# The gate of a two-expert adapter mixture: from a copied tile on two engines to VectorE reading PSUM

## Chip, cores and metric

The kernel runs on one core of a Trainium2 chip. A time is the device time of the whole program in microseconds (us); the kernel before takes 125.9 us, the median of three runs (125.78, 125.90, 126.79). Profiles are of single executions on the chip; the one of the kernel before has a span of 124.6 us from its first to its last instruction.

## The reference

Two parts follow each other. The first is a gated linear recurrence over 768 steps for 4 batches and 8 heads with 48 columns each; its output, with the heads laid side by side, is x with 3072 rows of 384. The second is a mixture of low-rank adapters: each row picks 2 of 8 experts.

```python
for t in range(S):
    state = alpha[:, :, t, :, None] * state + np.einsum('bhd,bhe->bhde', k[:, :, t], v[:, :, t])
    y[:, :, t] = np.einsum('bhd,bhde->bhe', q[:, :, t], state)
...
logits = x @ w_gate                                   # [3072, 8]
topk = np.argpartition(-logits, K, axis=1)[:, :K]     # K = 2
sel = np.take_along_axis(logits, topk, axis=1)
sel = sel - sel.max(-1, keepdims=True)
w = np.exp(sel)
w /= w.sum(-1, keepdims=True) + 1e-09
...                                                   # for each expert e of a row's two
z = x[mask] @ A[e]                                    # rank 16
delta[mask] += w[mask, k, None] * (z @ B[e])
...
return x + delta
```

## The kernel before

The sequence is cut into 24 chunks of 128 steps (6 for each batch); every stage below is a function of the chunk u. A planner inside the kernel gives each stage an engine and orders all stages of all chunks, so that chunks overlap; the weights in its table LEAD steer the order, and each engine then works its instructions off in that order. The stages outside the change, in a few words:

- `ln` (ScalarE): logarithm of alpha, two chunks at a time; `cum` (TensorE): its running sums; `eup`, `edn`, `edec` (ScalarE): their exponentials
- `kgm`, `qgm`, `vbc` (GpSimd): k and q scaled by these, v cast to bf16: 128x384 for each chunk, written as `kg`, `qg`, `vb`
- `tr` (TensorE) transposes `kg` and `qg` into PSUM, `kq` (VectorE) copies them out
- `at` (TensorE): scores within the chunk; `msk` (VectorE) multiplies them by the causal mask, `at_sb`, 128x1024
- `kv` (TensorE): the state; `sdm` (VectorE) decays it into `sdec`
- `yt` (TensorE): the chunk's output transposed, `xs` (ScalarE) copies it out
- `qs`, `av` (TensorE): the output once more, not transposed, added up in the bank `y`; `delta` adds the adapters' part there, `fin` (ScalarE) copies it out as `o`, and a DMA stores it.

The gate lies between `xs` and `zt`. One product with the weights of all experts beside the gate's gives 8 x 16 adapter columns and 8 logits in one PSUM tile; the rows below follow in this order.

```python
E = 8; R = 16; P = 128; NW = E * R + E
moep = ctx.enter_context(tc.tile_pool(name="moep", bufs=3))
# PSUM: one pool whose six banks (tag "m") are handed out in turn
# to cum, tr, kv, yt, z and y/zt of all chunks
...
def z(u):
    s["z"] = ps_s.tile([P, NW], F4, name="z", tag="m", bufs=6)
    for p in range(NP):
        nc.tensor.matmul(
            s["z"], s["xs"][:, p, :], W[:, p, :], start=(p == 0), stop=(p == NP - 1))

def zc(u):                                    # L565: all of z out to SBUF
    s["zc"] = moep.tile([P, NW], F4, name="zc")
    nc.scalar.copy(s["zc"], s["z"])

def gmx(u):                                   # L570: the eight logits in descending order
    s["mx"] = moep.tile([P, 8], F4, name="mx")
    nc.vector.max(s["mx"], s["zc"][:, E * R:NW])

def gdf(u):                                   # L575: less the largest
    s["df"] = moep.tile([P, E], F4, name="df")
    nc.vector.tensor_scalar(s["df"], s["zc"][:, E * R:NW], s["mx"][:, 0:1], None, ALU.subtract)

def gex(u):                                   # L580
    s["ex"] = moep.tile([P, E], F4, name="ex")
    nc.scalar.activation(s["ex"], s["df"], AF.Exp)

def gwu(u):                                   # L586: zero below the second largest; the sum to den
    s["wu"] = moep.tile([P, E], F4, name="wu")
    s["den"] = moep.tile([P, 1], F4, name="den")
    nc.vector.scalar_tensor_tensor(
        out=s["wu"], in0=s["zc"][:, E * R:NW], scalar=s["mx"][:, 1:2], in1=s["ex"],
        op0=ALU.is_ge, op1=ALU.mult, accum_out=s["den"])

def grd(u):                                   # L593
    s["rd"] = moep.tile([P, 1], F4, name="rd")
    nc.vector.reciprocal(out=s["rd"], in_=s["den"])

def gw(u):                                    # L598: the weights
    s["w"] = moep.tile([P, E], F4, name="w")
    nc.vector.tensor_scalar(s["w"], s["wu"], s["rd"][:, 0:1], None, ALU.mult)

def gzw(u):                                   # L603: each expert's 16 columns by its weight
    s["zw"] = moep.tile([P, E, R], F2, name="zw")
    nc.gpsimd.tensor_tensor(
        out=s["zw"], in0=s["zc"][:, 0:E * R].rearrange("p (e r) -> p e r", e=E),
        in1=_bc(s["w"][:, :], R), op=ALU.mult)

def zt(u):                                    # L611: transpose into the bank of y
    bank = ps_s.tile([P, 512], F4, name="y", tag="m", bufs=6)
    s["y"], s["zt"] = bank[:, 0:DM], bank[:, DM:512]
    nc.tensor.matmul(
        s["zt"], s["zw"].rearrange("p e r -> p (e r)"), ident[:, :],
        start=True, stop=False, skip_group_check=True)

def zs(u):                                    # L618
    nc.scalar.copy(s["zs"], s["zt"])
...
```

Of the kernel before, what the change touches and what calls it, by code (L numbers as in the profile page):

```python
# [9 lines left out]
ALU = mybir.AluOpType  # L10
# [3 lines left out]
F4 = mybir.dt.float32  # L14
# [5 lines left out]
E = 8  # L20
R = 16
P = 128
NP = H // 2
HP = 64
NW = E * R + E
# [8 lines left out]
def _bc(src: bass.AP, rep: int) -> bass.AP:  # L34
    aps = [list(x) for x in src.ap]
    return bass.AP(tensor=src.tensor, offset=src.offset, ap=aps + [[0, rep]])


def _bc_mid(src: bass.AP, reps) -> bass.AP:
# [14 lines left out]
    "gdf": ("DVE", 76, 160), "gex": ("ACT", 107, 232), "gwu": ("DVE", 268, 352),  # L54
    "grd": ("DVE", 71, 155), "gw": ("DVE", 76, 160), "gzw": ("POOL", 380, 430), "zt": ("PE", 57, 220),
    "zs": ("ACT", 147, 272), "delta": ("PE", 163, 330), "fin": ("ACT", 385, 485),
    "st": ("DMA", 655, 2455),
}
LEAD = {
    "vbc": -12.82, "ln": -79.7, "cum": -86.5, "edn": -48.18, "eup": 69.81, "edec": -28.78,  # L60
    "kgm": 82.51, "qgm": -38.95, "tr": -24.18, "kq": -54.99, "sdm": -7.62, "kv": 81.99,
    "at": -3.06, "msk": 19.28, "qs": 45.2, "av": -5.12, "xb": 0.5, "xt": 0.4, "xs": 19.13,
    "z": 54.23, "zc": -33.57, "gmx": -113.64, "gdf": -52.42, "gex": 27.38, "gwu": 83.15,
    "grd": -60.48, "gw": -7.12, "gzw": 60.4, "yt": 4.05, "zt": 33.97, "zs": 72.62,
    "delta": -14.68, "fin": -30.62, "st": 100,
}
CHAINS = (
    "ln cum eup kgm tr kq at msk yt xs z zc gmx gdf gex gwu grd gw gzw zt zs delta fin st",
    "cum edn qgm tr", "cum edec sdm kv", "kgm kv", "vbc kv", "sdm yt", "kq yt",
    "vbc yt", "zt qs av delta", "zt av",  # L70
)
# [2 lines left out]
    ("tr", "qgm", QRING), ("kv", "vbc", VRING), ("av", "vbc", VRING), ("at", "kq", 5), ("av", "kq", 5),  # L74
    ("msk", "at", 1), ("av", "msk", 4), ("z", "xs", 3), ("delta", "zs", 3), ("st", "fin", 5),
    ("qs", "sdm", SRING), ("kv", "sdm", 1), ("kgm", "cum", 3), ("qgm", "cum", 3), ("at", "tr", 5),
    ("av", "tr", 5), ("z", "yt", 3), ("gzw", "z", 3), ("delta", "zt", 3), ("st", "zt", 5),
    ("edec", "kv", -1), ("qs", "kv", SRING - 1), ("delta", "gzw", 3),
)
HOLDS = {  # L80
    "cum": (("eup", 0), ("edn", 0), ("edec", 0)), "tr": (("kq", 0),), "kv": (("sdm", 1),),
    "yt": (("xs", 0),), "z": (("zc", 0),), "zt": (("fin", 0),),
}
SLOTS = 6
READER = ("ln", "kgm", "qgm", "vbc")
# [174 lines left out]
def kernel(  # L260
# [11 lines left out]
    nc = tc.nc  # L272
# [8 lines left out]
    moep = ctx.enter_context(tc.tile_pool(name="moep", bufs=3))  # L281
# [64 lines left out]
    for n in early:  # L346
# [6 lines left out]
        out=suf, in_=suf, compare_op=ALU.is_gt, fill=0.0, base=0,  # L353
# [23 lines left out]
    for i in range(SRING):  # L377
# [8 lines left out]
        out=mask, in_=mask, compare_op=ALU.is_ge, fill=0.0, base=0,  # L386
# [4 lines left out]
    st = [dict() for _ in range(NU)]  # L391
# [167 lines left out]
            nc.tensor.matmul(  # L559
                s["z"], s["xs"][:, p, :], W[:, p, :], start=(p == 0), stop=(p == NP - 1))  # L560

    def zc(u):
        s = st[u]
        s["zc"] = moep.tile([P, NW], F4, name="zc")
        nc.scalar.copy(s["zc"], s["z"])  # L565

    def gmx(u):
        s = st[u]
        s["mx"] = moep.tile([P, 8], F4, name="mx")
        nc.vector.max(s["mx"], s["zc"][:, E * R:NW])  # L570

    def gdf(u):
        s = st[u]
        s["df"] = moep.tile([P, E], F4, name="df")
        nc.vector.tensor_scalar(s["df"], s["zc"][:, E * R:NW], s["mx"][:, 0:1], None, ALU.subtract)  # L575

    def gex(u):
        s = st[u]
# [3 lines left out]
    def gwu(u):  # L582
        s = st[u]
        s["wu"] = moep.tile([P, E], F4, name="wu")
        s["den"] = moep.tile([P, 1], F4, name="den")
        nc.vector.scalar_tensor_tensor(  # L586
            out=s["wu"], in0=s["zc"][:, E * R:NW], scalar=s["mx"][:, 1:2], in1=s["ex"],
            op0=ALU.is_ge, op1=ALU.mult, accum_out=s["den"])

    def grd(u):  # L590
# [1 line left out]
        s["rd"] = moep.tile([P, 1], F4, name="rd")  # L592
        nc.vector.reciprocal(out=s["rd"], in_=s["den"])  # L593

    def gw(u):
        s = st[u]
        s["w"] = moep.tile([P, E], F4, name="w")
        nc.vector.tensor_scalar(s["w"], s["wu"], s["rd"][:, 0:1], None, ALU.mult)  # L598

    def gzw(u):  # L600
        s = st[u]
        s["zw"] = moep.tile([P, E, R], F2, name="zw")
        nc.gpsimd.tensor_tensor(  # L603
            out=s["zw"], in0=s["zc"][:, 0:E * R].rearrange("p (e r) -> p e r", e=E),
            in1=_bc(s["w"][:, :], R), op=ALU.mult)

    def zt(u):
        s = st[u]
# [22 lines left out]
    def store(u):  # L631
# [3 lines left out]

    emit = dict(
        ld=ld, wcast=wcast, ln=ln, cum=cum, eup=eup, edn=edn, edec=edec, kgm=kgm, qgm=qgm, vbc=vbc,
        tr=tr, kq=kq, sdm=sdm, kv=kv, at=at, msk=msk, qs=qs, av=av, yt=yt, xs=xs, z=z, zc=zc,
        gmx=gmx, gdf=gdf, gex=gex, gwu=gwu, grd=grd, gw=gw, gzw=gzw, zt=zt, zs=zs, delta=delta, fin=fin,
        st=store)  # L640
    for n in order:
        if n not in early:
# [31 lines left out]
```

## Time and profile before

| engine | busy us | share of the span | instructions |
|---|---|---|---|
| TensorE, matmuls | 83.1 | 67% | 1312 |
| VectorE | 84.2 | 68% | 227 |
| GpSimd | 71.5 | 57% | 121 |
| ScalarE | 69.2 | 55% | 201 |

The table gives averages over the whole span. The first products run only when the first inputs have landed, so the shares of the stretch in which all engines work are higher than these; the prediction reads them stretch by stretch. In a row of the profile's groups, a name such as `df<-zc,mx` is an output and its inputs, the numbers behind the bar are the busy time of all instances in us and the mean of one in ns, and behind the second bar stands how long the engine was idle before them, with what ended most of that time. PE is TensorE, PEld its weight loads, DVE VectorE, ACT ScalarE, POOL GpSimd, SP the engine that issues most DMAs.

### The profile page before, as it was taken

The page shows a single profiled execution, that of the slowest core. Times are in us where ns is not written, and L with a number is a line of the kernel's source. Part 1 is how long each engine was busy: PE and PEld are TensorE (multiplying, and loading weights), DVE is VectorE, ACT ScalarE, POOL GpSimd, SP SyncE. Part 2 cuts the span into 40 slices and gives each one's busy share as a digit, 9 for nine tenths or more (in the row PEclk, how much of TensorE's full clock was granted, in tenths as well). Part 3 has the DMA queues.
Part 4 walks back from the last instruction along what each step waited for, and adds up shares of the span by engine and source line. Part 5 has one row for each costly group of instructions (what it writes and reads, how often), then busy time and mean ns, then how long its engine had stood idle before and what let it go on. Part 6 is the DMA issues. An engine that isn't in the chain of part 4 may idle for free.

```text
span 124.6 us, 3448 instructions
## 1 busy us (share of the span) xinstructions
PE 83.1 (67%) x1312; PEld 64.0 (51%) x1312; DVE 84.2 (68%) x227; ACT 69.2 (55%) x201; POOL 71.5 (57%) x121
## 2 busy tenths in 40 slices
PE   0000310994798689669896899689829997797750
PEld 0000210783566478447774676468618885575520
DVE  3000000589998877985898899999984599999520
ACT  0007910363279955614888767477694684455650
POOL 7400065979609479477447789772657597740310
PEclk9999999999999968976999999999985599999997
DMA  2976988998898949498969497977895510003051
GB/s 46 282 108 157 293 250 250 272 275 214 258 248 254 264 138 295 148 253 269 266 163 302 145 254 200 296 263 216 239 303 202 186 72 0 5 0 108 24 192 63
DMA packets 32064, 24.21 MB, mean 194 GB/s; under 512 B 4272, under 2 KB 32048, under 8 KB 32048
## 3 DMA queue, kind: packets, MB, share of 16 engines
q1 hardware_dynamic: 28288, 23.60, 63.9%
q10 hardware_dynamic: 3760, 0.41, 2.4%
q8 instruction: 10, 0.16, 0.6%
q14 instruction: 6, 0.05, 0.1%
HBM read 19.28 MB, written 4.72 MB: 193 GB/s over the span
## 4 chain that ended last, share of the span: by engine, by line
DVE 34%; PE 25%; DMA 12%; ACT 10%; SPq 9%; issue 4%; ACTq 1%; POOL 1%; POOLq 0%; DVEq 0%
DVE at_sb L512 13%; SPq L305 9%; DMA a_t<-in_alpha_dram 7%; DVE df L575 5%; DMA W_st<-in_moe_A_dram 5%; PE tr L474 4%; DVE sdec L461 4%; DVE kq L480 3%; DVE wu L586 3%; ACT xs L536 2%; PE yt L528 2%; PE z L559 2%; PE y L551 2%; PE y L622 2%; PE y L542 2%
## 5 line engine op out<-in xcount | busy, mean ns | idle before, releaser
L442 POOL TENSOR_TENSOR kg<-k_t,up 128x384 bf16<-128x384 f32 x24 | 23.9, 1003 | 22.9 <-DMA k_t<-in_k_dram 11.8
L480 DVE COPY kq<-tr 128x1024 bf16<-128x1024 bf16 x24 | 16.5, 686 | 23.6 <-PE tr L474 23.3
L512 DVE TENSOR_TENSOR at_sb<-at,mask 128x1024 bf16<-128x1024 f32 x24 | 29.3, 1219 | 1.6 <-PE y L551 0.7
L449 POOL TENSOR_TENSOR qg<-q_t,dn 128x384 bf16<-128x384 f32 x24 | 24.0, 1014 | 3.5 <-ACT dn L428 2.0
L603 POOL TENSOR_TENSOR zw<-zc,w 128x128 bf16<-128x128 f32 x24 | 9.5, 403 | 19.4 <-DVE w L598 8.7
L536 ACT CAST xs<-yt 128x512 bf16<-128x512 f32 x24 | 14.0, 582 | 7.5 <-PE yt L528 7.4
L408 PE MATMUL cum<-lg,suf 128*128 128x384 bf16 x24 | 9.0, 385 | 12.4 <-ACT lg L399 12.4
L423 ACT ACTIVATE up<-cum 128x384 f32<-128x384 f32 x24 | 11.1, 495 | 10.4 <-PE cum L414 10.4
L474 PE MATMUL tr<-ident,kg 128*128 128x128 bf16 x96 | 11.1, 249 | 3.9 <-POOL kg L442 3.9
L474 PE MATMUL tr<-ident,qg 128*128 128x128 bf16 x96 | 10.8, 244 | 3.7 <-POOL qg L449 3.7
L456 POOL CAST vb<-v_t 128x384 bf16<-128x384 f32 x24 | 12.0, 519 | 1.8 <-PE y L551 1.8
L559 PE MATMUL z<-W,xs 128*128 128x136 bf16 x96 | 10.5, 236 | 3.6 <-DVE W L333 1.8
L504 PE MATMUL at<-kq 48*128 48x128 bf16 x192 | 10.2, 229 | 3.2 <-DVE at_sb L512 2.7
L629 ACT COPY o<-y 128x384 f32<-128x384 f32 x24 | 10.9, 486 | 2.4 <-PE y L622 2.3
L528 PE MATMUL yt<-at_sb,vb 128*64 128x128 bf16 x192 | 10.4, 232 | 2.3 <-DVE at_sb L512 2.1
L575 DVE TENSOR_SCALAR df<-zc,mx 128x8 f32<-128x8 f32 x24 | 11.5, 485 | 0.4
L565 ACT COPY zc<-z 128x136 f32<-128x136 f32 x24 | 6.7, 281 | 8.8 <-PE z L559 8.5
L461 DVE TENSOR_TENSOR sdec<-kv,dec 128x384 bf16<-128x384 f32 x20 | 11.0, 548 | 1.0 <-PE kv L494 1.0
L428 ACT ACTIVATE dn<-cum 128x384 f32<-128x384 f32 x24 | 11.4, 518 | 0.0
L474 PEld LDWEIGHTS <-kg 128*128 128x128 bf16 x96 | 7.4, 110 | 5.9 <-POOL kg L442 4.0
L399 ACT ACTIVATE lg<-a_t 128x768 bf16<-128x768 f32 x12 | 10.2, 858 | 0.0
L580 ACT ACTIVATE ex<-df 128x8 f32<-128x8 f32 x24 | 4.9, 212 | 8.8 <-DVE df L575 8.7
(55 smaller groups left out, 168.5 us busy)
## 6 DMA issues: line engine op xcount, KB each, us to landing
out_dram<-o SPq DMA_DIRECT2D x24, 192.0 KB, 2.5
W_st<-in_moe_A_dram ACTq DMA_DIRECT2D x8, 24.0 KB, 4.9
B_st<-in_moe_B_dram ACTq DMA_DIRECT2D x1, 192.0 KB, 4.2
a_t<-in_alpha_dram SPq DMA_DIRECT2D x4, 0.2 KB, 7.9
k_t<-in_k_dram SPq DMA_DIRECT2D x4, 0.2 KB, 9.0
q_t<-in_q_dram SPq DMA_DIRECT2D x4, 0.2 KB, 8.9
v_t<-in_v_dram SPq DMA_DIRECT2D x4, 0.2 KB, 10.7
W_st<-in_moe_w_gate_dram ACTq DMA_DIRECT2D x2, 6.0 KB, 4.1
```

The source lines that it names most:

```text
L428: nc.scalar.activation(s["dn"].rearrange("p h d -> p (h d)"), s["cum"][:, 0:DM], AF.Exp, scale=-1.0)
L442: nc.gpsimd.tensor_tensor(out=s["kg"][:, :, 0:D], in0=batches[b][1][:, c], in1=s["up"], op=ALU.mult)
L449: nc.gpsimd.tensor_tensor(out=s["qg"][:, :, 0:D], in0=batches[b][2][:, c], in1=s["dn"], op=ALU.mult)
L456: nc.gpsimd.tensor_copy(out=s["vb"][:, :, 0:D], in_=batches[b][3][:, c])
L461: nc.vector.tensor_tensor(out=sdec[u % SRING].rearrange("p a b d -> p (a b) d")[:, :, 0:D], in0=st[u - 1].pop("kv").rearrange("p a b d -> ...
L474: nc.tensor.transpose(t[:, w, p, :], pair(src, p), ident[:, :])
L480: nc.vector.tensor_copy(out=s["kq"], in_=s["tr"])
L512: nc.vector.tensor_tensor(out=s["at_sb"].rearrange("p a b t -> p (a b) t"), in0=s["at"].rearrange("p a b t -> p (a b) t"), in1=_bc_mid(mas ...
L528: nc.tensor.matmul(s["yt"][HP * hh:HP * hh + HP, p, :], s["vb"][:, 2 * p + hh, :], s["at_sb"][:, hh, p, :], start=(c == 0 and p == 0), sto ...
L536: nc.scalar.copy(s["xs"], s["yt"])
L559: nc.tensor.matmul(s["z"], s["xs"][:, p, :], W[:, p, :], start=(p == 0), stop=(p == NP - 1))
L575: nc.vector.tensor_scalar(s["df"], s["zc"][:, E * R:NW], s["mx"][:, 0:1], None, ALU.subtract)
```

## The change

VectorE reads the logits, and then the adapter columns, straight from the PSUM tile `z`. The copy `zc` on ScalarE goes. The normalised weights `w` are no longer written: the product takes the unnormalised weights `wu` and the reciprocal `rd` in one instruction, and this instruction moves from GpSimd to VectorE[...]. It is meant to shorten the gate's chain by two links and to take work from ScalarE and GpSimd. The planner holds z's bank until `gzw` instead of until `zc`, and its weights LEAD are new for nearly all stages, so the order of emission differs throughout the kernel.

```diff
-    "z": ("PE", 240, 410), "zc": ("ACT", 153, 278), "gmx": ("DVE", 91, 175),
+    "z": ("PE", 240, 410), "gmx": ("DVE", 91, 175),
...
-    "grd": ("DVE", 71, 155), "gw": ("DVE", 76, 160), "gzw": ("POOL", 380, 430), "zt": ("PE", 57, 220),
+    "grd": ("DVE", 71, 155), "gzw": ("DVE", 258, 342), "zt": ("PE", 57, 220),
...
 LEAD = {
-    "vbc": -12.82, "ln": -79.7, "cum": -86.5, ...
+    "vbc": -52.68, "ln": -26.63, "cum": 56.89, ...
...
-    "ln cum eup kgm tr kq at msk yt xs z zc gmx gdf gex gwu grd gw gzw zt zs delta fin st",
+    "ln cum eup kgm tr kq at msk yt xs z gmx gdf gex gwu grd gzw zt zs delta fin st",
...
-    "yt": (("xs", 0),), "z": (("zc", 0),), "zt": (("fin", 0),),
+    "yt": (("xs", 0),), "z": (("gzw", 0),), "zt": (("fin", 0),),
...
-    def zc(u):
-        s = st[u]
-        s["zc"] = moep.tile([P, NW], F4, name="zc")
-        nc.scalar.copy(s["zc"], s["z"])
-
...
-        nc.vector.max(s["mx"], s["zc"][:, E * R:NW])
+        nc.vector.max(s["mx"], s["z"][:, E * R:NW])
...
-        nc.vector.tensor_scalar(s["df"], s["zc"][:, E * R:NW], s["mx"][:, 0:1], None, ALU.subtract)
+        nc.vector.tensor_scalar(s["df"], s["z"][:, E * R:NW], s["mx"][:, 0:1], None, ALU.subtract)
...
-            out=s["wu"], in0=s["zc"][:, E * R:NW], scalar=s["mx"][:, 1:2], in1=s["ex"],
+            out=s["wu"], in0=s["z"][:, E * R:NW], scalar=s["mx"][:, 1:2], in1=s["ex"],
...
-    def gw(u):
-        s = st[u]
-        s["w"] = moep.tile([P, E], F4, name="w")
-        nc.vector.tensor_scalar(s["w"], s["wu"], s["rd"][:, 0:1], None, ALU.mult)
-
     def gzw(u):
         s = st[u]
         s["zw"] = moep.tile([P, E, R], F2, name="zw")
-        nc.gpsimd.tensor_tensor(
-            out=s["zw"], in0=s["zc"][:, 0:E * R].rearrange("p (e r) -> p e r", e=E),
-            in1=_bc(s["w"][:, :], R), op=ALU.mult)
+        nc.vector.scalar_tensor_tensor(
+            out=s["zw"], in0=s["z"][:, 0:E * R].rearrange("p (e r) -> p e r", e=E),
+            scalar=s["rd"][:, 0:1], in1=_bc(s["wu"][:, :], R), op0=ALU.mult, op1=ALU.mult)
```

More of the change, by code (lines that the diff above doesn't have):

```diff
@@ L59 @@
 LEAD = {
[L60 to L65, printed above, removed]
+    "vbc": -52.68, "ln": -26.63, "cum": 56.89, "edn": 39.81, "eup": 21.91, "edec": -22.93,
+    "kgm": 25.06, "qgm": -48.73, "tr": 56.8, "kq": -24.41, "sdm": -13.3, "kv": -5.97,
+    "at": 120.74, "msk": -46.64, "qs": -121.83, "av": 19.7, "xb": 0.5, "xt": 0.4, "xs": -1.32,
+    "z": -75.7, "zc": -33.57, "gmx": 36.34, "gdf": -3.62, "gex": 91.18, "gwu": -50.53,
+    "grd": 20.25, "gw": -7.12, "gzw": -11.18, "yt": -15.31, "zt": 15.28, "zs": -110.93,
+    "delta": -25.33, "fin": -73.68, "st": 100,
 }
 CHAINS = (
-    "ln cum eup kgm tr kq at msk yt xs z zc gmx gdf gex gwu grd gw gzw zt zs delta fin st",
+    "ln cum eup kgm tr kq at msk yt xs z gmx gdf gex gwu grd gzw zt zs delta fin st",
     "cum edn qgm tr", "cum edec sdm kv", "kgm kv", "vbc kv", "sdm yt", "kq yt",
@@ L76 @@
     ("qs", "sdm", SRING), ("kv", "sdm", 1), ("kgm", "cum", 3), ("qgm", "cum", 3), ("at", "tr", 5),
-    ("av", "tr", 5), ("z", "yt", 3), ("gzw", "z", 3), ("delta", "zt", 3), ("st", "zt", 5),
+    ("av", "tr", 5), ("z", "yt", 3), ("delta", "zt", 3), ("st", "zt", 5),
     ("edec", "kv", -1), ("qs", "kv", SRING - 1), ("delta", "gzw", 3),
@@ L637 @@
         ld=ld, wcast=wcast, ln=ln, cum=cum, eup=eup, edn=edn, edec=edec, kgm=kgm, qgm=qgm, vbc=vbc,
-        tr=tr, kq=kq, sdm=sdm, kv=kv, at=at, msk=msk, qs=qs, av=av, yt=yt, xs=xs, z=z, zc=zc,
-        gmx=gmx, gdf=gdf, gex=gex, gwu=gwu, grd=grd, gw=gw, gzw=gzw, zt=zt, zs=zs, delta=delta, fin=fin,
+        tr=tr, kq=kq, sdm=sdm, kv=kv, at=at, msk=msk, qs=qs, av=av, yt=yt, xs=xs, z=z,
+        gmx=gmx, gdf=gdf, gex=gex, gwu=gwu, grd=grd, gzw=gzw, zt=zt, zs=zs, delta=delta, fin=fin,
         st=store)
```

## The prediction

> **What bounds the kernel now.** I read the page's first part (busy time by engine) for the balance, then busy time by stretch for where each engine is full, then the groups for the lines the change touches, and last the timeline around their longest instances.
>
> Busy time by stretch: stretch, length, then busy us of each engine, the granted TensorE clock, the DMA share and GB/s.
>
> ```profile
> 29.00:45.00 16.00, 11.59 (x202) 8.69 (x201) 14.49 (x40) 10.46 (x32) 10.22 (x16) 0.99 0.84 238
> 45.00:60.00 15.00, 12.55 (x184) 10.09 (x183) 11.15 (x27) 7.89 (x24) 10.67 (x16) 0.79 0.75 222
> 60.00:75.00 15.00, 12.43 (x226) 9.83 (x224) 13.35 (x35) 11.84 (x37) 9.84 (x14) 1.00 0.80 233
> 75.00:90.00 15.00, 13.26 (x227) 10.06 (x225) 14.81 (x39) 10.28 (x30) 10.10 (x16) 1.00 0.82 242
> 90.00:105.00 15.00, 11.35 (x167) 9.38 (x166) 11.32 (x26) 9.79 (x30) 10.48 (x17) 0.77 0.49 164
> 105.00:119.00 14.00, 11.70 (x201) 8.50 (x198) 12.22 (x45) 7.83 (x26) 5.74 (x10) 1.00 0.11 38
> ```
>
> The engines stand in the order TensorE, its weight loads, VectorE, ScalarE, GpSimd. The first 29 us are loading and start-up, which the change does not touch. Of the 90 us that follow, 60 (29 to 45, 60 to 90, 105 to 119) have VectorE busy 14.49 + 13.35 + 14.81 + 12.22 = 54.9 us, 91%; from 75 to 90 it is full. In the other 30 us (45 to 60, 90 to 105) TensorE's clock is 0.79 and 0.77, VectorE has a quarter of its time free, and the faster thing to have would be TensorE. So VectorE sets the pace in two thirds of the steady part. The DMA queues are busy but no engine waits for a load after start-up (the list of waits has DMA only under the first loads).
>
> The groups concerned (line, engine, operation, shapes, count | busy us, mean ns | idle before, releaser):
>
> ```profile
> L575 DVE TENSOR_SCALAR df<-zc,mx 128x8 f32<-128x8 f32 x24 | 11.5, 485 | 0.4
> L603 POOL TENSOR_TENSOR zw<-zc,w 128x128 bf16<-128x128 f32 x24 | 9.5, 403 | 19.4 <-DVE w L598 8.7 <-DVE df L575 5.0 <-ACT o L629 2.0
> L586 DVE SCALAR_TENSOR_TENSOR wu<-zc,mx,ex 128x8 f32<-128x8 f32 x24 | 7.6, 326 | 3.1 <-ACT ex L580 2.9
> L565 ACT COPY zc<-z 128x136 f32<-128x136 f32 x24 | 6.7, 281 | 8.8 <-PE z L559 8.5
> L598 DVE TENSOR_SCALAR w<-wu,rd 128x8 f32<-128x8 f32 x24 | 6.2, 268 | 1.6 <-POOL zw L603 0.5
> ```
>
> The surprise is df: eight elements per partition cost 485 ns on average, though the tile's own view gives 221 as its shortest and 300 as its median. The timeline says what the long ones sit beside:
>
> ```profile
> 69.02 1.97 POOL L449 TENSOR_TENSOR qg<-q_t,dn 128x384 bf16<-128x384 f32 x2
> ...
> 70.09 0.93 DVE L575 TENSOR_SCALAR df<-zc,mx 128x8 f32<-128x8 f32 x1
> ...
> 81.30 1.04 DVE L586 SCALAR_TENSOR_TENSOR wu<-zc,mx,ex 128x8 f32<-128x8 f32 x1
> 81.31 1.00 POOL L449 TENSOR_TENSOR qg<-q_t,dn 128x384 bf16<-128x384 f32 x1
> ```
>
> Start plus duration: df ends at 71.02 and GpSimd's pair at 70.99; wu ends at 82.34 and qg at 82.31. A tiny VectorE instruction lasts until GpSimd's 1.0 us product is through. Meanwhile at_sb, kq and sdec, which read PSUM, hold to their means (1219, 686, 548 ns) at all times.
>
> [...] So df with its tensor in PSUM, and wu with one input in PSUM, should leave the lock; kq's steady 686 ns fits.
>
> [...] From at_sb (1024 elements, 1219 ns) and sdec (384, 548): (1219 − 548)/640 = 1.048 ns an element and a fixed 548 − 402 = 146 ns, from PSUM. mx at its shortest, 144 ns for 8 elements from SBUF, leaves 144 − 8 = 136. I take the 10 ns[...].
>
> [...]
>
> **The change part by part.**
>
> Removed from VectorE:
> - w, 24 times: the next instruction starts 0.14 us after w (71.90 to 72.04), 24 × 0.14 = 3.4 us, and its lock share (268 − 231 median) × 24 = 0.9 us.
> - the lock in df: (485 − 225, the unlocked length) × 24 = 6.2 us.
> - the lock in wu: (326 − 227 median) × 24 = 2.4 us.
>
> Added to VectorE: gzw, 128 elements from PSUM with a per-partition scalar. 128 × 1.048 + 146 = 280 ns; the scalar costs what df's shortest has over mx's, 221 − 144 = 77; together about 357 ns. at_sb's 1219 ns leave 1.13 us from start to start (48.97 to 50.10), 0.09 overlapped, so gzw occupies 0.27 us, × 24 = 6.5 us. PSUM surcharge: 10 ns × 72 = 0.7 us.
>
> VectorE in sum: 12.9 − 7.2 = 5.7 us less, 84.2 to about 78.5.
>
> GpSimd loses 9.5 us of work, and its in-order queue loses the 19.4 us in which zw stood at its head while the kg and qg products behind it stood too. ScalarE loses 6.7 us of zc and the 8.8 us it was idle before it. TensorE's work is unchanged. The gate's chain loses the zc link and one hand-over; z's PSUM bank, given back by zc until now, is held until gzw. The emission order is also planned afresh (other LEAD weights), which I can't price.
>
> What of it lies on the path: the four full stretches hold 20 of the 24 df, with 2.19 + 2.16 + 2.40 + 1.70 = 8.45 us, of which 8.45 − 20 × 0.225 = 3.95 is lock. With 20/24 of the rest: 3.95 + 2.0 + 3.6 − 6.0 = 3.55 us less VectorE there. TensorE has 49.0 us of those 60, so it becomes the next limit; I let three quarters through: 2.7 us. In the two slow-clock stretches VectorE isn't the bound, but the chain that ended last passes through df there in pieces of 0.65, 0.97 and 0.68 us; I give 0.4 us. In the tail, the last chunk's max starts 0.30 us earlier without zc (117.21 to 117.51), and gzw can start where w started (119.09) and end at 119.45, where zw ended at 119.87: 0.7 us together. For the longer hold of the bank I take off 0.6 us. 2.7 + 0.4 + 0.7 − 0.6 = 3.2 us: 125.9 − 3.2 = 122.7 us.
>
> **Rivals.**
>
> 1. VectorE gets fuller. Counted without locks the change adds work: 0.27 − 0.14 = +0.13 us a chunk, + 0.7 us: 3.8 us in all. If most long df and wu are waits for something else than GpSimd, or the locks fall on times when nothing hangs on VectorE, the time goes to 127 to 129. For it: VectorE is the bound. Against: the matched ends, and that the long df lie in the full stretches too.
>
> 2. The PSUM bank takes the place of the lock. Six banks are handed out in turn to cum, tr, kv, yt, z and zt; 5 × 24 + 20 = 140 tiles in 90 us, one per 0.64 us, so a bank comes round after about 3.9 us. z is held under 1 us now (71.85 to the end of its copy, 72.62). From mx to the end of w the timeline of VectorE shows 1.6 to 5.6 us, mostly near 2.4, with five chunks over 4 us. If gates stay that long, TensorE's next tile waits for gzw: several waits of 1 to 2 us, and 125 to 128. For it: in-order queues on both sides. Against: those five long gates are ones where other VectorE work was placed inside the gate, and the order is planned anew with z held until gzw.
>
> 3. TensorE, or its clock, holds the pace. It has 72.9 us of the 90 and no less work. Then the faster VectorE only makes it wait: 124.5 to 125.5. For it: the two stretches near 0.78. Against: the full clock in the other 60 us.
>
> 4. All 5.7 us and the freed GpSimd come through, with kg and qg running ahead into the batch changes (VectorE waited 0.84 us for tr at 48.36, 0.71 at 98.22): 118 to 120.
>
> **Range and chances.** Centre 122.7; 119.3 where rival 4 comes mostly true, 126.3 where the bank or the PSUM surcharge eats the gain. The line for faster by 2% is 123.4, close to the centre, and rival 3 ends above it: 0.58. Within 2% (123.4 to 128.4): 0.28. Slower: 0.14, for the bank with an unlucky order.
>
> **What would show it.** df near 230 ns and wu near 225 on average, no instance near 1 us; gzw near 350 ns; VectorE near 78.5 us busy, GpSimd near 62, ScalarE near 62.5. The 75 to 90 us part no longer full on VectorE. A wait of TensorE for zw at lines other than zt's would show the bank's price. I am wrong if df stays long with its tensor in PSUM[...], if gzw takes 500 ns, or if the time falls while VectorE's busy time does not.

## The result, and the profile after

The changed kernel takes 119.53 us (median of four, 118.44 to 120.75) where the kernel before takes 125.94. The ratio is 0.945, with a 95% interval of 0.937 to 0.953. Beside other runs, on another occasion, the same kernel came to 0.924 (0.917 to 0.930) of before. The two intervals do not meet, so a difference of up to 2% between runs of different occasions carries no weight below. Ratios compare undisturbed executions of both kernels, so a ratio can differ a little from that of two medians.

The time lies inside the stated range (119.3 to 126.3), but the gain is twice the 3.2 us forecast: 6.4 us by the medians, 6.9 by the ratio. First the operations. The busy times of the engines after:

```profile
PE 79.2 (68%) x1312; PEld 60.5 (52%) x1312; DVE 77.7 (67%) x227; ACT 63.6 (54%) x177; POOL 62.0 (53%) x97
```

VectorE has 77.7 us (78.5 was forecast), GpSimd 62.0 (62), ScalarE 63.6 (62.5). TensorE has 79.2 us where it had 83.1, with the same 1312 instructions; its mean granted clock is 0.948 in this execution and 0.939 in that of before. The groups of the gate, in the same columns as before:

```profile
L593 DVE SCALAR_TENSOR_TENSOR zw<-z,rd,wu 128x128 bf16<-128x128 f32 x24 | 7.9, 345 | 0.2
L581 DVE SCALAR_TENSOR_TENSOR wu<-z,mx,ex 128x8 f32<-128x8 f32 x24 | 5.1, 221 | 2.9 <-ACT ex L575 2.7
L570 DVE TENSOR_SCALAR df<-z,mx 128x8 f32<-128x8 f32 x24 | 5.0, 220 | 0.3
L565 DVE MAX8 mx<-z 128x8 f32<-128x8 f32 x24 | 4.1, 170 | 3.3 <-PE z L559 3.0
```

df fell from 485 to 220 ns on average and its longest instance is 226 ns, where it was 1040. wu fell from 326 to 221. The product takes 345 ns (357 forecast). mx is 11 ns longer out of PSUM than out of SBUF (159 before). All four are close to what was worked out.

Busy time by stretch after (TensorE, its weight loads, VectorE, ScalarE, GpSimd; then clock, DMA share, GB/s):

```profile
29.00:45.00 16.00, 12.72 (x189) 9.45 (x187) 13.58 (x37) 9.97 (x26) 9.52 (x12) 0.79 0.87 242
45.00:60.00 15.00, 13.48 (x255) 10.94 (x256) 13.70 (x38) 10.44 (x30) 9.50 (x14) 1.00 0.86 252
60.00:75.00 15.00, 13.28 (x235) 10.07 (x233) 13.35 (x38) 10.01 (x32) 11.76 (x15) 1.00 0.77 229
75.00:90.00 15.00, 11.47 (x214) 8.83 (x210) 11.78 (x45) 11.08 (x32) 7.43 (x10) 1.00 0.78 228
90.00:105.00 15.00, 12.46 (x202) 9.65 (x200) 12.60 (x27) 6.64 (x21) 9.20 (x13) 0.89 0.46 151
105.00:117.00 12.00, 7.16 (x123) 4.98 (x120) 5.91 (x28) 5.82 (x17) 0.00 (x0) 0.91 0.27 100
```

The part from 75 to 90 us had VectorE full (14.81 of 15); now it has 11.78, and no engine is full there. Something else is waited for. The chain that ended last, by engine, before and then after:

```profile
DVE 34%; PE 25%; DMA 12%; ACT 10%; SPq 9%; issue 4%; ACTq 1%; POOL 1%; POOLq 0%; DVEq 0%
```

```profile
PE 31%; DMA 28%; DVE 16%; ACT 13%; issue 4%; ACTq 1%; SPq 1%; POOL 1%; DVEq 0%
DMA q_t<-in_q_dram 9%; DMA v_t<-in_v_dram 7%; DMA out_dram<-o 6%; DMA W_st<-in_moe_A_dram 5%; PE tr L474 5%; DVE at_sb L512 4%; PE z L559 4%; PE yt L528 4%; ACT lg L399 3%; DVE kq L480 3%; ACT xs L536 3%; PE at L504 3%; PE y L612 2%; PE yt L523 2%; ACT dn L428 2%
```

VectorE's share of the chain halves. The DMAs' share more than doubles, but part of that is the start: before's chain comes through the queue that issues the loads (SPq, 9%), after's through the landing of the first q (9%). New in the middle of the kernel are two pieces, a store's landing of 7.45 us and the last v's of 7.86 us. The waits of after that have to do with DMAs or with the moved product (who, for what: us in total, times, longest):

```profile
POOL kg L442 <- DMA k_t<-in_k_dram: 12.5, 2, 11.7
ACT o L619 <- DMA out_dram<-o: 5.6, 3, 3.1
POOL qg L449 <- DMA q_t<-in_q_dram: 4.2, 2, 2.6
...
PE y L601 <- DVE zw L593: 2.0, 4, 0.8
...
POOL vb L456 <- DMA v_t<-in_v_dram: 0.7, 1, 0.7
```

One k_t and one q_t wait are those of the start, as before. The rest is new: GpSimd waits 2.6 us for q in the middle of the kernel and 0.7 us for the last v, and ScalarE can't write an output tile because an earlier store from it has not landed. TensorE waits for zw only at L601, the transpose that reads it; at no other line does it wait for the bank that z now holds longer.

### The profile page after: what moved, and what is told of

Read it like the earlier page. It is cut to its first block, busy times and chain, and to the rows that moved or that the text cites. A ratio compares the mean times of both kernels' runs of the same rounds, so it can differ in the third digit from the quotient of the medians.

```text
span 116.7 us, 3365 instructions
## 1 busy us (share of the span) xinstructions
PE 79.2 (68%) x1312; PEld 60.5 (52%) x1312; DVE 77.7 (67%) x227; ACT 63.6 (54%) x177; POOL 62.0 (53%) x97
## 4 chain that ended last, share of the span: by engine, by line
PE 31%; DMA 28%; DVE 16%; ACT 13%; issue 4%; ACTq 1%; SPq 1%; POOL 1%; DVEq 0%
DMA q_t<-in_q_dram 9%; DMA v_t<-in_v_dram 7%; DMA out_dram<-o 6%; DMA W_st<-in_moe_A_dram 5%; PE tr L474 5%; DVE at_sb L512 4%; PE z L559 4%; PE yt L528 4%; ACT lg L399 3%; DVE kq L480 3%; ACT xs L536 3%; PE at L504 3%; PE y L612 2%; PE yt L523 2%; ACT dn L428 2%
## 5 line engine op out<-in xcount | busy, mean ns | idle before, releaser
L474 PE MATMUL tr<-ident,kg 128*128 128x128 bf16 x96 | 10.4, 237 | 4.2 <-POOL kg L442 4.2
L504 PE MATMUL at<-kq 48*128 48x128 bf16 x192 | 10.2, 229 | 3.3 <-DVE at_sb L512 2.4
L559 PE MATMUL z<-W,xs 128*128 128x136 bf16 x96 | 10.1, 236 | 3.3 <-ACT xs L536 1.9
L528 PE MATMUL yt<-at_sb,vb 128*64 128x128 bf16 x192 | 10.2, 229 | 0.0
L399 ACT ACTIVATE lg<-a_t 128x768 bf16<-128x768 f32 x12 | 10.1, 855 | 0.0
L474 PEld LDWEIGHTS <-qg 128*128 128x128 bf16 x96 | 7.3, 108 | 4.1 <-POOL qg L449 4.1
L504 PEld LDWEIGHTS <-kq 48*128 48x128 bf16 x192 | 6.1, 98 | 6.1 <-issue 2.2
L474 PEld LDWEIGHTS <-kg 128*128 128x128 bf16 x96 | 6.3, 104 | 5.4 <-POOL kg L442 4.4
L559 PEld LDWEIGHTS <-xs 128*128 128x128 bf16 x96 | 6.4, 102 | 5.2 <-ACT xs L536 2.7
```

The source lines that it names most:

```text
L399: nc.scalar.activation(lgs[(u // G) % 2][:, :, :, 0:D], batches[b][0][:, c:c + G], AF.Ln)
L474: nc.tensor.transpose(t[:, w, p, :], pair(src, p), ident[:, :])
L504: nc.tensor.matmul(t[:, hh, p, :], s["kq"][rows, 0, p, :], s["kq"][rows, 1, p, :], start=True, stop=True)
L528: nc.tensor.matmul(s["yt"][HP * hh:HP * hh + HP, p, :], s["vb"][:, 2 * p + hh, :], s["at_sb"][:, hh, p, :], start=(c == 0 and p == 0), sto ...
L559: nc.tensor.matmul(s["z"], s["xs"][:, p, :], W[:, p, :], start=(p == 0), stop=(p == NP - 1))
```

## The experiments

The change has three parts that can be had singly: the lock (here the name for what the prediction's timelines show of a df and a wu, 0.93 and 1.04 us long, each ending within 0.03 us of a GpSimd product; df and wu reading PSUM take it off), the product (on VectorE, w gone), and the order. The first four runs part them. Theory 1 was that the operations made the gain, theory 2 that the order made half or more, theory 3 that each order fits only its own operations.

**The order alone.** Tables of after (stages, LEAD, chains, holds), functions of before:

```diff
 def gmx(u):
+    zc(u)
...
     nc.vector.reciprocal(out=s["rd"], in_=s["den"])
+    gw(u)
```

> The operations of before in the order of after: zc is emitted just ahead of each max, w just behind each reciprocal. If the operations made the gain (theory 1): 124.5 to 127, df still near 480 ns. If the new order made half of it or more (theory 2): 121 to 123. If each order only fits its own operations (theory 3): above 128.

Measured: 129.75 us, ratio 1.027 (1.015 to 1.040), in the range of theory 3. The order is no gain in itself. df is 375 ns here and not near 480: in this order five df last over 400 ns, in before eleven. In it the old product on GpSimd has a poor place; its row:

```profile
L605 POOL TENSOR_TENSOR zw<-zc,w 128x128 bf16<-128x128 f32 x24 | 9.7, 402 | 35.2 <-DVE rd L594 10.8 <-DVE df L576 9.7 <-DVE wu L587 4.2
```

GpSimd stands idle for 35.2 us ahead of zw, against 19.4 before. This order was planned for a product that isn't in GpSimd's queue, and the places of zc and w in it were chosen for this run.

**The operations alone.** Functions of after, tables of before, the places of zc and w left empty:

```diff
-        if n not in early:
+        if n not in early and n[0] not in ("zc", "gw"):
```

> The operations of after in the order of before, with the places of zc and w left empty. Theory 1 (operations): 119 to 121. Theory 2 (order): 122 to 124, the 3.2 us that the prediction found. Theory 3 (fit): 123 to 126, with TensorE waiting for banks that z holds.

Measured: 121.07 us, ratio 0.958 (0.947 to 0.970), 5.2 us by the ratio (3.8 to 6.7) and nearer to theory 1. Its busy times:

```profile
PE 82.6 (69%) x1312; PEld 64.0 (53%) x1312; DVE 77.5 (64%) x227; ACT 63.8 (53%) x177; POOL 62.3 (52%) x97
```

By the ratios the operations carry most of the gain in the old order; what the clock may have to do with it stands under the next run.

**The lock alone.** Before, with two operands changed; zc, w and the product on GpSimd stay:

```diff
-        nc.vector.tensor_scalar(s["df"], s["zc"][:, E * R:NW], s["mx"][:, 0:1], None, ALU.subtract)
+        nc.vector.tensor_scalar(s["df"], s["z"][:, E * R:NW], s["mx"][:, 0:1], None, ALU.subtract)
...
-            out=s["wu"], in0=s["zc"][:, E * R:NW], scalar=s["mx"][:, 1:2], in1=s["ex"],
+            out=s["wu"], in0=s["z"][:, E * R:NW], scalar=s["mx"][:, 1:2], in1=s["ex"],
```

> Order and copy zc of before, but df and wu take the logits from the bank of z; the product stays on GpSimd. df 220 ns, wu 221, VectorE's busy time 8 to 9 us less. If nearly all VectorE time in the gate comes through to the end: 119 to 121. If three quarters of two thirds do, as predicted: 121.5 to 122.5. If TensorE holds the pace: 124.5 to 126.

Measured: 121.93 us, ratio 0.962 (0.948 to 0.975): 4.8 us by the ratio. Its busy times and groups:

```profile
PE 79.5 (67%) x1312; PEld 61.5 (52%) x1312; DVE 77.3 (66%) x227; ACT 68.3 (58%) x201; POOL 71.4 (60%) x121
...
L598 DVE TENSOR_SCALAR w<-wu,rd 128x8 f32<-128x8 f32 x24 | 8.0, 344 | 1.6 <-POOL zw L603 0.5
...
L575 DVE TENSOR_SCALAR df<-z,mx 128x8 f32<-128x8 f32 x24 | 5.2, 221 | 0.4
L586 DVE SCALAR_TENSOR_TENSOR wu<-z,mx,ex 128x8 f32<-128x8 f32 x24 | 5.2, 222 | 4.7 <-ACT ex L580 4.5
```

Two operands, with the same instructions in the same order on the same engines, take 264 ns off df and 104 off wu. That the long instances go with the operand is thus shown; and in before all eleven df over 400 ns last until a GpSimd instruction ends, nine times a kg or qg, once vb and once zw. Part of the time comes back elsewhere: w, which still reads and writes SBUF, grows from 268 to 344 ns. In before already one w takes 0.71 us, from 88.55, beside a pair of kg that runs from 88.23 to 90.19 us; its shortest has 0.225. VectorE's busy time falls by 84.2 - 77.3 = 6.9 us, and by the ratio 4.8 us of it, 0.7 for each, reach the end.

How much of the 4.8 us is the clock's is not settled. The four executions of this run took 119.72, 121.09, 122.76 and 124.27 us at a mean granted TensorE clock of 0.969, 0.957, 0.949 and 0.935. Before beside it took 124.55 to 125.04 us at 0.945 and 124.84 and 125.66 at 0.934. At about equal clock the lock alone is thus worth 1 to 2 us, and in the same way the operations alone some 2.8 (122.01 us at 0.953, 123.55 at 0.925, where before has 126.38 at 0.920). Whether taking the lock off brings the higher clock, or the clock differed for other reasons, no run shows. The gain of the whole change does not hang on it: after took 119.57 us at 0.936 and 118.44 at 0.948.

**The product alone.** Before, with gzw as in after and w left out; df and wu read the copy:

> Order and copy zc of before, df and wu still from the copy, but the product on VectorE out of z's bank, w gone. VectorE has 6.5 - 4.3 = 2.2 us more of its own work, GpSimd 9.5 less. If VectorE's time decides: 126.5 to 128. If GpSimd's queue behind zw decided: 122 to 124, and df stays near 480 ns.

Measured: 127.45 us, ratio 1.020 (1.010 to 1.031). With the lock left in, the move is a loss of 2.5 us; the first rival of the prediction counts 3.8. Its row and df's say why.

```profile
L575 DVE TENSOR_SCALAR df<-zc,mx 128x8 f32<-128x8 f32 x24 | 11.6, 486 | 0.5
...
L603 DVE SCALAR_TENSOR_TENSOR zw<-z,rd,wu 128x128 bf16<-128x128 f32 x24 | 7.8, 341 | 0.2
```

df stays at 486 ns although GpSimd has 9.1 us less to do (62.4 busy). That fits before, where nine of the eleven long df end with a kg or qg, of 1.0 us each, and only one with zw.

**The same parts in the new order.** The run with the order alone, plus the two operands of the lock run; and plus the product instead of them:

> As the run with the order of after and the operations of before, but df and wu take the logits from z's bank: in this order too the lock alone is removed. If the lock is the cause whatever the order: 4 to 6 us under that run's 128.6, thus 123 to 124.5, df 220 ns. If the order was the obstacle there: above 126.5.

> The order of after and its product on VectorE, but the copy zc is back and df and wu read it, so the lock is back too. If the lock costs what it cost in the order of before: 5 to 8 us over after, 124.5 to 127.5, df 375 to 490 ns. If the copy in the chain matters little and the lock also: 120 to 122.

Measured: 125.71 us, 0.991 (0.988 to 0.995), without the lock, between my two alternatives and a gain of 3.6 points over the order alone, as in the old order. With the product and the lock: 122.76 us beside 126.18, 0.973 by the medians and without an interval, so only roughly (its four executions take 120.65 to 123.35 us). In this order the product is worth some 5 points with the lock in place, where it cost 2 in the old one. The second of my alternatives for this run, that the lock and the copy hardly matter here, is the closer one; df is 281 ns there, not 485.

| | nothing | lock off | product | both |
|---|---|---|---|---|
| order of before | 1 | 0.962 | 1.020 | 0.958 |
| order of after | 1.027 | 0.991 | 0.973 (medians) | 0.945, again 0.924 |

Taking the lock off gains clearly in three of the four pairs, and in the fourth (product, order of after) only roughly. What the product is worth depends on the order, and the order on the product.

**Is VectorE still the limit?** After with df computed three times, two of them unread; and after without df, where ScalarE takes the exponential of logit plus largest logit (the normalised weights are the same, but large logits would overflow):

```diff
+        for i in range(2):
+            j = moep.tile([P, E], F4, name=f"j{i}")
+            nc.vector.tensor_scalar(j, s["z"][:, E * R:NW], s["mx"][:, 0:1], None, ALU.subtract)
```

```diff
-        nc.scalar.activation(s["ex"], s["df"], AF.Exp)
+        nc.scalar.activation(s["ex"], s["z"][:, E * R:NW], AF.Exp, bias=s["mx"][:, 0:1])
...
-        if n not in early:
+        if n not in early and n[0] != "gdf":
```

> After, with df computed three times (two copies that nobody reads): 2 x 24 x 0.14 = 6.7 us more on VectorE, nothing on another engine, no lock. If VectorE's time reaches the end nearly whole: 124.5 to 127. If three quarters of two thirds of it do, as the prediction had it: 122.5 to 123.5. If TensorE sets the pace of after: 119.5 to 121.

> After without df: ScalarE takes exp(logit + largest logit) straight from z's bank, which leaves the normalised weights as they are but gives up the protection against overflow for large logits. VectorE loses 24 x 0.14 to 0.2 = 3.4 to 4.8 us and the chain one link. If VectorE still decides: 115 to 117. If TensorE sets the pace of after: 118.5 to 119.5.

Measured: 0.936 (0.929 to 0.942) with 4.9 us more on VectorE (82.6 busy), 0.931 (0.922 to 0.940) with 4.0 us less (73.7). Both lie where after lies (0.924 to 0.945), the first of them below all three ranges that I had given. My expectation that VectorE would still decide fell: a span of 9 us of VectorE work changes nothing that can be seen. The chain of after pointed to the loads, so the next four runs have to do with loads left out.

**Fewer loads.** q is loaded for the first batch only, and the later batches read that tile; the same on before; then two further subtractions for each chunk, on before and on the kernel with fewer loads:

```diff
 def load(b, i, c, eng):
+    if i == 2 and b > 0:
+        return
...
-        out=s["qg"][:, :, 0:D], in0=batches[b][2][:, c], in1=s["dn"], op=ALU.mult)
+        out=s["qg"][:, :, 0:D], in0=batches[0][2][:, c], in1=s["dn"], op=ALU.mult)
```

> After, with q loaded for the first batch only (the other three batches read that tile again, so their outputs are left wrong): 3 of 16 loads of some 4.6 us of DMA time each are left out. If the loads and the stores behind them set the pace of after: 113 to 116.5, and no engine waits for a landing store. If TensorE sets it: 118.5 to 119.5, as after.

> The same on before. If before is held by VectorE and its locks, as argued: 124.5 to 126, no gain. If loads held before too: 121 to 123.

> Before, with two more subtractions for each chunk that read the logits from PSUM and so take no lock: 6.7 us more on VectorE at most, nothing elsewhere. If VectorE's time as such sets the pace of before: 130 to 133. If what the locks cost was their length inside the gate's chain and not VectorE's total: 125.5 to 128.

> After with q loaded once, and with df computed three times: does VectorE's time count once the loads are out of the way? If so: 4 to 7 us over the run with fewer loads. If TensorE is the limit behind the loads: within 1.5 us of that run.

Measured: after with fewer loads 113.56 us, ratio 0.900 (0.893 to 0.908); before with fewer loads 1.002 (0.999 to 1.005). So the loads cap after and not before. In after with fewer loads no engine waits for a load behind the start, and the last v is first read at 91.94 us, 3.4 us earlier than in after, where it was read as soon as it had landed.

```profile
91.94 0.97 POOL L458 CAST vb<-v_t 128x384 bf16<-128x384 f32 x2
```

The busy times of the two kernels with more on VectorE, first before, then after with fewer loads:

```profile
PE 84.7 (66%) x1312; PEld 65.0 (51%) x1312; DVE 88.9 (69%) x275; ACT 69.8 (54%) x201; POOL 71.4 (56%) x121
```

```profile
PE 78.0 (68%) x1312; PEld 59.6 (52%) x1312; DVE 82.8 (72%) x275; ACT 64.1 (55%) x177; POOL 62.0 (54%) x97
```

Before: 88.9 - 84.2 = 4.7 us more on VectorE make 130.21 us, ratio 1.034 (1.024 to 1.043), 4.2 us. VectorE was the limit there; 0.9 of each added microsecond reaches the end. After with fewer loads: 82.8 - 77.4 = 5.4 us more make 0.925 (0.915 to 0.935), against 0.900 a gain lost of 0.0247 x 126.1 = 3.1 us, below the 4 to 7 that I expected. Behind the loads VectorE counts again, at 0.6. With all loads it counted nothing. The two limits lie close together and do not add up: from 113.56 us the loads alone lead to 118 to 119.5, the added work alone to 116.83 and both together to 117.49, and with both no engine waits for a load or a store behind the start. My range of 130 to 133 for before was a little high because two subtractions took 4.7 us and not 6.7.

What makes the loads late stays open. The 16 loads of alpha, k, q and v and the 24 stores go out on one queue, SP's. In after the last v is issued at 87.39 us, behind twelve stores; with the operations alone, in the old order, at 81.27 us, behind eleven. Full DMAs (their share is 0.77 to 0.87 in the stretches from 29 to 90 us) or the place that the new order gives the load would both fit, and no run parts them.

**The order, with the loads out of the way.** The operations alone and the lock alone, each with fewer loads:

> The operations of after in the order of before, with q loaded for the first batch only. After with fewer loads took 113.56. If the new order is worth something by itself on the compute side: 115.5 to 118. If the order only hid the loads better: 113 to 114.5.

> The order of before, the product on GpSimd, only df and wu off the lock, and q loaded once. If the loads capped the gain of the lock at 4.8 us: 117 to 119. If not: 120.5 to 122, as without that. Against the run with all operations and fewer loads, the difference is what the product's move is worth without the loads: -0.5 to 0.5 by VectorE's time alone would be +1.5 to +2.

Measured: 0.953 (0.942 to 0.963) and 0.949 (0.930 to 0.968). Neither differs clearly from its run with all loads (0.958, 0.962); the first took 119.73 us, more than either of my ranges for it. In the old order no cap by the loads is seen. After with fewer loads has 0.900, so with the new operations the new order is worth about 5 points on the compute side. This does not hang on the clock: at 0.963 to 0.976 the old order takes 119.41 to 119.73 us and the new one 113.52 to 114.15. The loads let 1.3 (0.958 to 0.945) to 3.5 (0.958 to 0.924) of these points through; the lower end of that is within the intervals.

**Which part of the DMAs.** Eight output tiles in place of five, alone and without df:

```diff
-    outp = ctx.enter_context(tc.tile_pool(name="outp", bufs=5))
+    outp = ctx.enter_context(tc.tile_pool(name="outp", bufs=8))
```

> After with eight output tiles in place of five, so that the copy out of y no longer waits for a store that lies behind the loads (5.6 us in three waits, one of 7.45 us on the chain of after). If that wait reached the end: 117 to 118.5. If the loads' own arrival holds the pace: 119 to 120.

> Without df, as above, and with eight output tiles: the candidate for a kernel better than after. If the two add up: 115 to 116.5. If the loads hold it: 117 to 118, as without df.

Measured: 0.927 (0.907 to 0.947) and 0.936 (0.915 to 0.956), too wide. Then after and the first of these beside each other, in five rounds:

> After, unchanged, beside the run with eight output tiles on the same chip: 0.94 to 0.95 of before if the first measurement holds.

> After with eight output tiles: 0.92 to 0.93 of before and clear of after, if the wait for stores reaches the end; within 0.5% of after if the loads hold the pace either way.

Measured: 0.924 (0.917 to 0.930) and 0.924 (0.917 to 0.931); for after I had expected 0.94 to 0.95. The wait for the stores is gone from the list of the run with eight tiles, and the waits for loads remain:

```profile
POOL qg L449 <- DMA q_t<-in_q_dram: 2.2, 2, 1.7
POOL vb L456 <- DMA v_t<-in_v_dram: 0.6, 1, 0.6
```

So no cost of the store wait, 6.4% of the chain of after, is seen in the ratios. That it lay beside time in which the loads would have been waited for fits, but isn't shown: the medians of all six executions are 118.26 and 116.99 us, which leaves room for about 1 us. No version came out clearly better than after.

## Why the prediction was wrong in its size

**The durations held.** Each duration and each engine's busy time was within a few per cent, and the run that changes only two operands shows that df and wu are no longer held when they read PSUM (485 to 221 ns, 326 to 222). Why they are held with the tensor in SBUF is not shown: the runs tell when the held instructions end and which operand frees them, and the word lock stands for no more than that. No larger fixed cost of a PSUM source appears: mx takes 170 ns out of PSUM and 159 out of SBUF, 11 more where 10 were worked out, and df and wu take 220 and 221, where from SBUF the shortest df had 221 and the median wu 227. That a PSUM surcharge could eat the gain, as the range had it, was my estimate and not shown by a trace.

**The term that was mis-sized is the new order**, which the prediction put at nothing ("planned afresh ..., which I can't price"). With the operations of before it is worth -2.7 points, with those of after +1.3 to +3.5 with all loads, and 5 without the loads' cap. By the ratios some 1.7 to 4.4 us of the gain are thus the order's. At about equal clock an estimate is 3 us: some 6 for the whole change (119.65 us at 0.934, where before has 125.42 to 126.47 at 0.935), less the 2.8 of the operations alone. A term that can't be priced is not zero: it was written into the sum as if it were.

**The share of VectorE's time** may be a second one. "The four full stretches", "three quarters" and 0.4 us for the other stretches made 3.1 us of 5.7, or 0.54 for each. Measured by the ratios: 0.9 when work was added to before (0.6 to 1.2), and when the lock came off 0.7. The lock alone, 6.9 us less, gives 4.8 instead of 3.7 us; its interval (3.1 to 6.6 us) holds both, and at about equal clock it is less than either. The operations alone, 5.2 us by the ratio, pass the whole forecast of 3.2 without any new order, but at about equal clock they fall short of it. So that this share was too low is not proven. That the two stretches with the slow clock spared VectorE less than I took it is possible and not shown; of the three pieces of df that I counted to them, the one of 0.97 us starts at 89.26 us and lies almost wholly in the full stretch ahead.

**The product's price.** I charged 6.5 + 0.7 us to VectorE for it, against 4.3 for w, 1.6 us at the end by my share. In the old order and without the lock it cost nothing (0.962 to 0.958, not resolved), with the lock 2 points. VectorE's time says why it was so cheap: 77.3 us with the lock alone, where w had grown to 8.0, and 77.5 with the product, which takes 7.8, in its place. What GpSimd's freed queue and the shorter chain added, no run tells.

**The bank** (0.6 us taken off): no wait of TensorE for gzw outside its own transpose (2.0 us in four waits there). Nothing was due.

**The tail** (0.7 us): the last at_sb starts at 113.67 of a span of 124.6 before, and at 106.52 of 116.7 after:

```profile
113.67 1.23 DVE L512 TENSOR_TENSOR at_sb<-at,mask 128x1024 bf16<-128x1024 f32 x1
```

```profile
106.52 1.22 DVE L512 TENSOR_TENSOR at_sb<-at,mask 128x1024 bf16<-128x1024 f32 x1
```

124.6 - 113.67 = 10.9 and 116.7 - 106.52 = 10.2 us are left: 0.7 us, as worked out. In the old order it is the same: 120.3 - 110.22 = 10.1 with the operations alone, 118.0 - 107.13 = 10.9 with the lock alone. These are single executions.

**The rivals.** The first (VectorE fuller) is what happens when the product moves and the lock stays. The second did not come. The third said that TensorE holds the pace; a limit beside VectorE did appear, but it is the loads. The fourth, that the whole of the time and the freed GpSimd come through, named 118 to 120, where the result lies; but the operations that it counts on make 121.07 in the old order, so its range was met partly by luck. I had read that no engine waits for a load, which was true, and not asked how far ahead of their use the loads land. The last v of before is issued at 84.14 us; with the 10.7 us that v takes to land in the median, an estimate for its landing is 95. GpSimd first reads it at 101.38:

```profile
101.38 1.42 POOL L456 CAST vb<-v_t 128x384 bf16<-128x384 f32 x3
```

Six microseconds of room. In after the chain shows the read right at the landing:

```profile
87.39 7.86 DMA v_t<-in_v_dram
95.31 0.51 POOL vb L456
```

and from there the last batch needs 116.7 - 95.3 = 21.4 us to the end. With fewer loads it is 111.9 - 91.9 = 20.0, and with eight output tiles, where v is read at 93.70 right at its landing, 113.9 - 93.7 = 20.2. So in the new order the end follows this read after 20 to 21.4 us, and in after the read can't come ahead of the landing.

## What to carry to other kernels

A tiny VectorE instruction whose mean lies far above its shortest (485 against 221 ns here) deserves a look at what GpSimd does beside it: set start plus duration of both next to each other, and let it read its tensor operand from PSUM if that is there anyway (here that took df to 221 ns). Before sizing a gain, measure for each input the time between its landing and its first read; here the gain ended where that room ended. Where a change brings a new order of emission, the order is a part of the change with a size of its own, and it is told apart by running the new operations in the old order. Look at the granted clock beside each time: where kernels differ in both, compare executions of about equal clock too.

## What the runs showed of the hardware

In before, a df of eight elements for each partition took 1040 ns, where the shortest has 221, and ended at 90.21 us, GpSimd's pair of kg at 90.19; with the tensor in PSUM no df of after takes over 226. With df and wu reading PSUM and the rest as in before, w went from 268 to 344 ns. Not every instruction that reads SBUF is held: a rd and a mx of before, at 88.29 and 88.36 us, took 0.15 us each beside the first of that pair of kg, where the w at 88.55 took 0.71. What decides between them was not shown. And a wait that stands on the chain that ended last with 7.45 us (a store's landing) could be removed without a gain in the ratio (0.924 and 0.924); up to about 1 us may hide in the scatter.
